# Casting the second piece of w_in on GpSimd and VectorE, half each, instead of on GpSimd alone

## The chip, the cores and the metric

One core of a Trainium2 chip. The time is device microseconds (us) of one execution. The profile is one execution taken by the hardware profiler; its span (first to last instruction) is some 1.8 us shorter than the time. A run that is over 1.5% above the fastest of its kernel would count as slow.

## The reference

Linear attention (softmax of q over the head dimension, softmax of k over the sequence), then a feed-forward pair with exact GELU. All inputs are float32.

```python
kv = np.einsum('bhsd,bhse->bhde', k_s, v)                 # q, k, v: (8, 8, 576, 64)
attn = np.einsum('bhsd,bhde->bhse', q_s, kv)
x = attn.transpose(0, 2, 1, 3).reshape(4608, 512)
h = x @ w_in                                               # w_in: (512, 2048)
out = (0.5 * h * (1 + erf(h / sqrt(2)))) @ w_out           # w_out: (2048, 512)
```

## The kernel before

In this kernel TensorE multiplies w_in in bf16, so w_in must be cast. It arrives in five pieces of columns (256, 256, 512, 512, 512), each staged in float32 as 128 partitions x 4 blocks of 128 rows (in this kernel also called head pairs, since x comes out of the attention by head pairs). GpSimd casts the first piece block by block and the second in two halves of two blocks; VectorE casts the rest, one block per instruction.

```python
    wi_cols = [256, 256, 512, 512, 512]

    def cast_wi(i, w, eng):
        n = wi_cols[i]
        r = n // 128
        o = wi_bf[:, :, wi_off[i]:wi_off[i] + n].rearrange("p d (c m) -> p d c m", c=r)
        w = w[:, :, 0:n].rearrange("p d (m c) -> p d c m", c=r)
        if eng == "p":
            for h in range(2):
                nc.gpsimd.tensor_copy(out=o[:, 2 * h:2 * h + 2], in_=w[:, 2 * h:2 * h + 2])   # L428
        else:
            for c in range(NDM):
                nc.vector.tensor_copy(out=o[:, c], in_=w[:, c])                                # L431
    ...
    for dm in range(NDM):
        cast_wi_dm(0, wi[0], dm, nc.gpsimd)          # L439, four casts of 128x256
    ...                                              # x of the first batch, its evacuation to xT
    cast_wi(1, wi[1], "p")
    ...
    h_phase(0, {0: [lambda: cast_wi(2, wi[2], "v")], ...}, groups={0: 2, 4: 4, 8: 4}, ...)
```

`h_phase` computes tiles of 128 columns of h. Tiles 0 and 1 (first piece) are interleaved, eight matmuls. Tiles 2 and 3 (second piece) follow one by one, four matmuls each, one per block. Tiles 4 to 7 read the third piece. All matmuls with w_in are at L327, those with w_out at L355.

The softmax here doesn't subtract the row's maximum and nothing guards it: scores larger than these inputs give would overflow.

Of the kernel before, what the change touches and what calls it, by code (L numbers as in the profile page):

```python
# [16 lines left out]
def kernel(  # L17
# [16 lines left out]
    nc = tc.nc  # L34
# [43 lines left out]
    def table(func):  # L78
        nc.scalar.activation(out=scr[:, 1:2], in_=scr[:, 0:1], func=func)  # L79
# [225 lines left out]
    def x_all(b):  # L305

        for hp in range(HP):
            pool, tag = (psum_h, "h") if hp < 3 else (psum_a, "a")
            x_tile(b, hp, pool, tag)
        x_mm(b, 0)  # L310
        x_mm(b, 1)
        for hp, eng in ((0, "s"), (2, "v"), (1, "s"), (3, "v")):
            x_evac(b, hp, eng)

    def x_evac(b, hp, eng="v"):
        ps = st[b][f"x{hp}"]
        if eng == "v":
            nc.vector.tensor_copy(out=st[b]["xT"][:, hp, :], in_=ps)  # L318
        else:
            nc.scalar.copy(out=st[b]["xT"][:, hp, :], in_=ps)  # L320
# [88 lines left out]
    def load_wi(i):  # L409

        w = wst.tile([128, NDM, 512], FP32, tag="w")
        n = wi_cols[i]
        src = moe_w_in[:, wi_off[i]:wi_off[i] + n].rearrange("(c p) f -> p c f", p=128)
        d = NDM // wi_parts[i]
        for c in range(0, NDM, d):
            nc.sync.dma_start(out=w[:, c:c + d, 0:n], in_=src[:, c:c + d])
        return w
# [3 lines left out]
    def cast_wi(i, w, eng):  # L421
        n = wi_cols[i]
        r = n // 128
        o = wi_bf[:, :, wi_off[i]:wi_off[i] + n].rearrange("p d (c m) -> p d c m", c=r)
        w = w[:, :, 0:n].rearrange("p d (m c) -> p d c m", c=r)
        if eng == "p":
            for h in range(2):
                nc.gpsimd.tensor_copy(out=o[:, 2 * h:2 * h + 2], in_=w[:, 2 * h:2 * h + 2])  # L428
        else:
            for c in range(NDM):  # L430
                nc.vector.tensor_copy(out=o[:, c], in_=w[:, c])  # L431
# [53 lines left out]
    wi = [load_wi(i) for i in range(5)]  # L485
# [43 lines left out]
    x_mm(0, 1)  # L529
    x_evac(0, 2, "s")  # L530
    x_evac(0, 3)
    cast_wi(1, wi[1], "p")
    table(AF.Gelu)

    def ybank():
# [4 lines left out]
    def a2bank(i):  # L540
# [3 lines left out]

    h_phase(0, {
        0: [lambda: cast_wi(2, wi[2], "v")],
        2: [lambda: cast_wi(3, wi[3], "v")],
        6: [lambda: cast_wi(4, wi[4], "v")],
        9: [lambda: cast_wo(0, wo[0])],
# [91 lines left out]
    for c in range(2, B + 1):  # L641
# [19 lines left out]
        if c < B:  # L661
            w = [lambda c=c: x_all(c + 1)]
# [34 lines left out]
```

## Time and profile before

| | before |
|---|---|
| time, first 3 runs | 279.69 us median, 279.55 to 280.07 |
| profiled execution | 279.73 us, span 277.9 us |
| TensorE busy | 271.6 us, 98% of the span |
| GpSimd's two casts of the second piece | 0.64 and 1.05 us |
| TensorE's gap before tile 2's third matmul | 0.435 us, of which 0.216 is the usual spacing |

How to read it: in the groups and the timeline a row is start, length, engine, line, operation, tiles, shapes and count; a bracket at the end gives idle time of the engine and what ended it. PE is TensorE's matmuls, PEld its weight loads, DVE is VectorE, POOL is GpSimd. L431 is line 431 of that run's kernel, so an edit moves the numbers a little: the casts of the third piece are L431 before and L432 in the changed kernel. The chain of waits follows the last instruction back through what released each step; only time on this chain can be won.

### The profile page before, as it was taken

How to read it: one execution, taken by the hardware profiler on the slowest of the kernel's cores; microseconds unless marked ns; L12 is line 12 of the kernel's file. 1: busy time of each engine (PE TensorE's matmuls, PEld its weight loads, DVE VectorE, ACT ScalarE, POOL GpSimd, SP SyncE). 2: the span in 40 equal slices, each digit the busy share in tenths (PEclk: the TensorE clock that was granted, in tenths of full speed). 3: DMA queues.
4: the chain of work that ended last, by engine and by line, in shares of the span. 5: the costliest groups of instructions: out<-in, count | busy, mean ns of one | idle time of the engine just before them, and what ended most of it. 6: DMA issues, size and time to landing. Idle time of an engine off the chain costs nothing.

```text
span 277.9 us, 4563 instructions
## 1 busy us (share of the span) xinstructions
PE 271.6 (98%) x1918; PEld 126.1 (45%) x1918; DVE 100.6 (36%) x153; ACT 157.9 (57%) x246; POOL 33.4 (12%) x27
## 2 busy tenths in 40 slices
PE   7799999999999999999999999999999999999995
PEld 3444454444444444444444444444444444444443
DVE  2876574319743540093008400651015200130012
ACT  4867675789377816791569246943683363136400
POOL 1530041002020220014000500050005000000000
PEclk9999999999999999999999999999999999999999
DMA  7999999963992148712981199117502500220033
GB/s 249 396 400 429 398 400 407 398 251 100 297 341 60 68 107 255 294 38 87 247 346 41 43 234 389 46 49 189 115 0 75 151 2 0 75 78 0 0 78 77
DMA packets 44981, 50.10 MB, mean 180 GB/s; under 512 B 20385, under 2 KB 29857, under 8 KB 44705
## 3 DMA queue, kind: packets, MB, share of 16 engines
q1 hardware_dynamic: 44560, 49.39, 53.2%
q10 hardware_dynamic: 400, 0.43, 0.6%
q8 instruction: 15, 0.25, 0.4%
q14 instruction: 6, 0.04, 0.1%
HBM read 36.70 MB, written 9.44 MB: 166 GB/s over the span
## 4 chain that ended last, share of the span: by engine, by line
PE 93%; DMA 4%; POOL 1%; ACTq 0%; SPq 0%; issue 0%; DVE 0%
PE ps L355 44%; PE ps L327 43%; DMA w<-in_moe_w_in_dram 2%; DMA touch<-in_moe_w_in_dram 2%; PE kv L199 2%; PE ps L294 1%; PE ps L380 1%; PE pair L327 1%; POOL wi_bf L428 1%; POOL wi_bf L439 1%; PE ps L299 0%; PE tp L255 0%; ACTq L482 0%; PE ps L255 0%; ACTq L101 0%; SPq L103 0%
## 5 line engine op out<-in xcount | busy, mean ns | idle before, releaser
L327 PE MATMUL ps<-xT,wi_bf 128*128 128x512 bf16 x568 | 125.1, 379 | 0.1
L355 PE MATMUL ps<-wo_bf,g 128*128 128x512 bf16 x560 | 124.2, 379 | 0.0
L333 ACT ACTIVATE g<-ps 128x512 bf16<-128x512 f32 x142 | 83.6, 598 | 67.0 <-PE ps L327 66.9
L327 PEld LDWEIGHTS <-wi_bf 128*128 128x128 bf16 x576 | 56.1, 98 | 68.2 <-POOL wi_bf L428 0.5
L355 PEld LDWEIGHTS <-g 128*128 128x128 bf16 x560 | 53.9, 98 | 64.3 <-issue 0.4
L363 DVE COPY y_sb<-ps 128x512 f32<-128x512 f32 x33 | 22.6, 686 | 81.0 <-PE ps L355 80.6
L238 POOL TENSOR_TENSOR e<-e,recq 128x2048 bf16<-128x2048 bf16 (+1 forms) x9 | 25.7, 2856 | 175.3 <-DVE recq L237 147.2
L162 DVE CAST v_aug<-f 128x576 bf16<-128x576 f32 x24 | 16.4, 745 | 48.8 <-DMA f<-in_v_dram 48.8
L236 DVE TENSOR_REDUCE qsum<-e 128x16 f32<-128x1024 bf16 (+1 forms) x13 | 21.1, 1620 | 13.9 <-ACT e L145 13.9
L320 ACT CAST xT<-ps 128x512 bf16<-128x512 f32 x18 | 9.9, 588 | 28.1 <-PE ps L294 18.1
L145 ACT ACTIVATE e<-f 128x512 bf16<-128x512 f32 (+1 forms) x42 | 20.5, 556 | 3.2 <-DMA f<-in_q_dram 3.0
L150 ACT ACTIVATE ek<-f 128x2304 bf16<-128x2304 f32 (+1 forms) x10 | 17.2, 1728 | 0.6 <-DMA f<-in_k_dram 0.6
L318 DVE CAST xT<-ps 128x512 bf16<-128x512 f32 x17 | 11.0, 685 | 17.0 <-PE ps L294 14.1
L79 ACT ACT_TABLE_LOAD x9 | 11.5, 1283 | 2.8 <-issue 2.6
L472 PE MATMUL ps<-zeros 128*128 128x512 f32 x14 | 8.6, 779 | 1.4 <-DVE zeros L497 1.4
L145 ACT ACT_TABLE_LOAD x7 | 9.0, 1283 | 0.1
L431 DVE CAST wi_bf<-w 128x512 bf16<-128x512 f32 x12 | 7.4, 648 | 2.2 <-DMA w<-in_moe_w_in_dram 2.0
L199 PEld LDWEIGHTS <-ek 64*64 64x64 bf16 x576 | 6.4, 105 | 2.7 <-issue 0.6
L199 PE MATMUL kv<-v_aug,ek 64*64 64x65 bf16 x576 | 6.8, 193 | 0.5 <-POOL v_aug L162 0.5
L238 DVE TENSOR_TENSOR e<-e,recq 128x1024 bf16<-128x1024 bf16 x4 | 6.3, 1565 | 0.1
L472 PEld LDWEIGHTS ps<-zeros 128*128 128x128 f32 x14 | 3.5, 258 | 5.7 <-issue 4.3
L294 PE MATMUL ps<-qT,kvc 64*64 64x512 bf16 x62 | 5.4, 389 | 0.4 <-DVE kvc L218 0.4
(37 smaller groups left out, 49.9 us busy)
## 6 DMA issues: line engine op xcount, KB each, us to landing
out_dram<-y_sb SPq DMA_DIRECT2D x32, 256.0 KB, 2.4
f<-in_k_dram SPq DMA_DIRECT2D x6, 1152.0 KB, 10.2
f<-in_v_dram SPq DMA_DIRECT2D x6, 1152.0 KB, 11.8
f<-in_q_dram SPq DMA_DIRECT2D x6, 1024.0 KB, 7.2
w<-in_moe_w_in_dram SPq DMA_DIRECT2D x6, 512.0 KB, 8.6
f<-in_v_dram SPq DMA_DIRECT2D x8, 288.0 KB, 6.6
f<-in_q_dram SPq DMA_DIRECT2D x4, 512.0 KB, 8.8
w<-in_moe_w_out_dram SPq DMA_DIRECT2D x2, 1024.0 KB, 11.6
```

The costliest lines, as they stand in the source:

```text
L79: nc.scalar.activation(out=scr[:, 1:2], in_=scr[:, 0:1], func=func)
L145: nc.scalar.activation(out=dst[:, i], in_=src[:, u], func=AF.Exp)
L150: nc.scalar.activation(out=ek[b % 2][:, i:i + n], in_=st[b]["kf"][:, i:i + n].rearrange("p x (n d) -> p x n d", n=NS), func=AF.Exp,)
L162: eng.tensor_copy(out=o, in_=i)
L199: nc.tensor.matmul(st[b]["kv"][hp][c, 0:D + 1], ek[b % 2][pr, hp, n, :], v_aug[b % 2][pr, hp, n, 0:D + 1], start=(n == 0), stop=(n == NS - 1),
L236: nc.vector.reduce_sum(out=qsum, in_=eq[:, :, hs, :], axis=AX.X)
L238: eng.tensor_tensor(out=eq[:, :, hs, :], in0=eq[:, :, hs, :], in1=recq.unsqueeze(3).to_broadcast([128, J, w, D]), op=ALU.mult,)
L327: nc.tensor.matmul(ps, wi_bf[:, dm, t * 128:(t + 1) * 128], st[c]["xT"][:, dm, :], start=(dm == 0), stop=(dm == NDM - 1),)
L333: nc.scalar.activation(out=st[c]["g"][:, t, :], in_=ps, func=AF.Gelu)
L355: nc.tensor.matmul(ps, st[c]["g"][:, t, j * 128:(j + 1) * 128], wo_bf[:, t, :], start=(t == 0), stop=(t == NDF - 1),)
L363: nc.vector.tensor_copy(out=y_sb, in_=ps)
L472: nc.tensor.matmul(ps, z[:, 0:128], z, start=True, stop=True)
```

## The change

The intent is to have the second piece ready sooner: two engines cast it side by side, and VectorE does its half before it turns to the third piece.

```diff
-        if eng == "p":
-            for h in range(2):
-                nc.gpsimd.tensor_copy(out=o[:, 2 * h:2 * h + 2], in_=w[:, 2 * h:2 * h + 2])
+        if eng == "pv":
+
+            nc.gpsimd.tensor_copy(out=o[:, 0:2], in_=w[:, 0:2])
+            nc.vector.tensor_copy(out=o[:, 2:4], in_=w[:, 2:4])
...
-    cast_wi(1, wi[1], "p")
+    cast_wi(1, wi[1], "pv")
```

## The prediction

> **What bounds the kernel now.** I read the page first: which engine is busy, what the chain of waits holds.
>
> ```profile
> span 277.9 us, 4563 instructions
> PE 271.6 (98%) x1918; PEld 126.1 (45%) x1918; DVE 100.6 (36%) x153; ACT 157.9 (57%) x246; POOL 33.4 (12%) x27
> ...
> PE 93%; DMA 4%; POOL 1%; ACTq 0%; SPq 0%; issue 0%; DVE 0%
> PE ps L355 44%; PE ps L327 43%; DMA w<-in_moe_w_in_dram 2%; DMA touch<-in_moe_w_in_dram 2%; PE kv L199 2%; PE ps L294 1%; PE ps L380 1%; PE pair L327 1%; POOL wi_bf L428 1%; POOL wi_bf L439 1%; PE ps L299 0%; PE tp L255 0%; ACTq L482 0%; PE ps L255 0%; ACTq L101 0%; SPq L103 0%
> ```
>
> TensorE (PE) is busy 98% of the span and is 93% of the chain. Vector, Scalar and GpSimd engines have room. The only compute on the chain that is not TensorE's is GpSimd's: the casts of w_in at L439 and L428, 1% each. L428 is the line that the change touches. So next the chain of waits in order of time, between 10 and 30 us (start, length, what):
>
> ```profile
> 13.27 0.05 issue
> 13.32 1.48 POOL wi_bf L439 x4
> 14.80 1.59 POOL wi_bf L428 x2
> 16.40 0.05 issue
> 16.45 5.35 PE ps L327 x24
> ```
>
> GpSimd casts the first piece of w_in in four instructions, then the second in two, and when the last of these ends TensorE goes on. From 16.45 us to the end the chain names TensorE alone (in its part after 46 us no other engine has over 0.1%, until the last copy). Hence what is won at 16.45 us is won at the end, as long as no other wait takes the place; what is won elsewhere is worth nothing. But the chain's 1.59 us for L428 is not what can be won: TensorE worked most of that time. How long it stood still, the timeline says, read in short windows so that rows are not merged:
>
> ```profile
> 16.01 0.38 PE L327 MATMUL ps<-xT,wi_bf 128*128 128x512 bf16 x1
> ...
> 16.44 0.55 PEld L327 LDWEIGHTS <-wi_bf 128*128 128x128 bf16 x4 [0.55 <-POOL wi_bf L428]
> ...
> 16.45 0.39 PE L327 MATMUL ps<-xT,wi_bf 128*128 128x512 bf16 x1
> ```
>
> Undisturbed, these matmuls start 0.216 us apart (ten starts from 14.06 to 16.01 give 1.95 / 9; 48 in the 10.36 us of the chain after 28.27 give the same). The one after 16.01 should have started at 16.226 and started at 16.445. **The stall is 0.22 us.** The 0.55 us before the weight load is mostly the usual idle time of a loader that is one matmul ahead. Which matmul is it? Tiles 0 and 1 are run interleaved, eight matmuls; then tile 2, one head pair after another. The stalled one is tile 2's third: head pair 2, the first to read the second half of the second piece. Last, the casts around it:
>
> ```profile
> 14.20 0.69 DVE L318 CAST xT<-ps 128x512 bf16<-128x512 f32 x1
> ...
> 14.75 0.64 POOL L428 CAST wi_bf<-w 128x512 bf16<-128x512 f32 x1
> ...
> 15.25 0.62 DVE L431 CAST wi_bf<-w 128x512 bf16<-128x512 f32 x1 [0.36 <-DMA w<-in_moe_w_in_dram]
> ...
> 15.34 1.05 POOL L428 CAST wi_bf<-w 128x512 bf16<-128x512 f32 x1
> ...
> 15.89 0.97 DVE L431 CAST wi_bf<-w 128x512 bf16<-128x512 f32 x1
> ```
>
> VectorE finishes its last evacuation of xT at 14.89 and waits until 15.25 for the third piece. GpSimd's second cast takes 1.05 us where its first took 0.64, and VectorE's next takes 0.97 where the median of the 12 is 0.62.
>
> **What the Trainium skill says.** (1) "SBUF — State Buffer", section "Who interferes with whom": VectorE in a two-port mode and GpSimd hold a shared port pair as an exclusive lock for the whole instruction; who issues first has it, the other blocks fully. "Copy" and "cast" are listed as able to enter such a mode. The trace agrees: the second GpSimd cast overlaps a VectorE cast that began 0.09 us before it and ends 0.40 us later than its sibling would; the VectorE cast after it is longer by 0.35 us. (2) "VectorE: DVE Perf Modes", "Mode 2×_2P — use both read ports for one tensor": source and destination in SBUF, and an outermost dimension that is even. The new half has two head pairs outermost, so I take it for a two-port cast too. (3) "Perfetto Trace Analysis", "GPSIMD Engine Instruction": a GpSimd span is unreliable, and the spacing of starts is better. Starts here are 0.59 us apart, so 0.64 is not far off, and TensorE's release 0.05 us after the recorded end of 16.39 backs that end.
>
> **The change part by part.** The order of instructions on each engine, compared: GpSimd has one L428 cast instead of two; VectorE has one more cast of 128x512, between the xT evacuation and the 12 casts of L431; the others are unchanged, except that tile 2's third weight load now waits for VectorE. No bytes, transfers or matmuls change.
>
> Removed: GpSimd's second cast, 1.05 us, of which about 0.40 us is waiting. Its first stays where it was, 14.75 to 15.39, so tile 2's first two matmuls, from 15.79 on, have their weights in time.
>
> Added: one VectorE cast. The second piece landed at 14.62 by the record of its transfer, so the cast can start when VectorE is free, about 14.91. Alone it takes 0.62 us, to 15.53. But GpSimd has had the ports since 14.75, so I expect it to be held, as the VectorE cast at 15.89 was: that one ended 0.47 us after GpSimd's end (16.86 less 16.39). The same after 15.39 gives 15.86; with 0.05 us for the semaphore, 15.91. The matmul is due at 16.226, and in the trace before it started with its weight load (16.44 and 16.45), so I count a stall only from there. The whole stall goes, with 0.3 us to spare; with 0.1 if the load has to keep its usual lead of one matmul, at 16.01.
>
> Moved: the casts of the third piece. The first starts near 15.88 instead of 15.25, but no GpSimd cast is left to collide with: three casts of 0.62 us end near 17.75, where they ended at 17.40. The fourth waits for its data (landed 18.50) in both kernels. TensorE reads the first in tile 4, which it reaches after six more matmuls: 16.226 + 6 x 0.216 = 17.52, one us after it is ready (16.50). The second is ready at 17.12 and wanted at 18.38, the third at 17.75 and wanted at 19.25. All are hidden.
>
> Transfers: the staging buffer of the second piece comes free earlier, but the transfer that reuses it is issued at 16.64, right after another one landed at 16.58, not after the cast at 16.39. I expect it to stay there. The next, at 19.17, follows the third piece's fourth cast, which doesn't move.
>
> Then the waits further on, where a TensorE that is 0.22 us early might meet something that didn't move. Fourth piece: ready 20.23 for 20.98. Last piece: ready 24.49 for about 25.1. First cast of w_out: ready 27.19 for 28.05. Transposes of the second batch: VectorE's normalisation ends 38.02, TensorE comes at 38.41. Its v: GpSimd's last cast ends 42.84, TensorE comes at 43.19. The smallest margin is some 0.35 us, above the 0.22 us that is taken from it. So nothing should absorb the gain.
>
> Sum: 279.69 - 0.22 + 0 = **279.47 us**, 0.08% less.
>
> **Rivals.**
> A. VectorE's half ends late: the port pair changes hands more slowly, or its 64-column pattern is slower than L431's. If it ended at 16.30 instead of 15.86, TensorE would go on at 16.35 instead of 16.45, and the gain would be 0.1: 279.6. For it: both overlapping casts in this trace came out long. Against: their added 0.35 to 0.40 us is in my sum already.
> B. VectorE gets the ports first, or both get half speed. If VectorE holds them from 14.91 to 15.53, GpSimd's half ends 0.52 us later (as at 16.39, after 15.87), at 16.05; with the semaphore 16.10, and tile 2's first matmul, due at 15.79, stalls by 0.31. The 0.22 is saved and 0.31 lost: 279.8. For it: only 0.16 us separates the two starts, and GpSimd's depends on a transfer landing at 13.27. Against: GpSimd starts first in this trace.
> C. The gain is made and lost again at a wait tied to transfers, which are saturated until 55 us: 279.69. For it: many transfers land just ahead of use between 30 and 45 us. Against: the margins above.
> D. The extra VectorE work delays the third piece's casts until VectorE bounds the stretch. It would need over 1 us of delay, and the sum shows 0.35; nothing in the profile speaks for it.
>
> **Range and chances.** I give the main line 0.7 (279.47), A 0.12, B 0.06 and C 0.12. The weighted mean is 0.7 x 279.47 + 0.12 x 279.6 + 0.06 x 279.8 + 0.12 x 279.69 = 279.54; I say 279.5, between it and the main line. Three runs of the kernel before spread over 0.52 us, more than twice the effect, so the range is set by that spread: 279.1 to 279.9. Two per cent is 5.6 us, and the whole of the touched stretch, from the first cast to the resumed matmul, is 3.1 us; so faster by 2% is shut out, and slower by 2% would need a failure that no rival contains. Chances: 0.01, 0.98, 0.01.
>
> **What would show it.** Right: the matmuls of tile 2 run 0.216 us apart with no gap near 16.2; the page's chain has no L428 entry; the VectorE cast of L429 starts near 14.9 and ends at 15.8 to 15.9, longer than 0.62 us, while GpSimd's L428 cast keeps its 0.64; the L431 casts after it take 0.62 each; TensorE's chain from there on is unbroken and the span is 277.7. Wrong: a weight load that waits for L429 or for GpSimd at 15.6; L428 over 0.9 us long; a new gap between 17 and 45 us; or a span at 277.9 although the gap at 16.2 is gone, in which case the first displaced wait after it is the one to look for.

(The weighted mean in it should read 279.53; the slip of 0.01 changes nothing.)

## The result

| | before | changed |
|---|---|---|
| median of 6 runs | 279.59 us (279.49 to 280.07) | 279.54 us (279.43 to 279.83) |
| ratio of the means | | 0.9997, 95% interval 0.9984 to 1.001 |
| profiled span | 277.9 us | 277.7 us |
| first matmul with w_in to first with w_out | 14.054 us | 13.824 us |
| from there to the last matmul | 246.203 us | 246.207 us |

A ratio is the mean time of one kernel's fast runs over the mean of the other's fast runs of the same rounds, so it is not quite the ratio of the medians. Every interval below is a 95% interval of such a ratio.

The last two rows are differences of start times of single matmuls in the two traces. I use them below because they leave out the front of the kernel: over all 14 profiles TensorE's first matmul with w_in came anywhere between 14.02 and 14.27 us.

From the page of the changed kernel, the busy times and the chain of waits:

```profile
PE 269.6 (97%) x1890; PEld 126.3 (45%) x1918; DVE 100.7 (36%) x154; ACT 157.8 (57%) x246; POOL 32.4 (12%) x26
...
PE 93%; DMA 4%; issue 1%; POOL 0%; DVE 0%; SPq 0%
PE ps L327 44%; PE ps L355 43%; DMA f<-in_v_dram 2%; PE kv L199 2%; PE ps L294 2%; DMA f<-in_q_dram 1%; PE ps L380 1%; PE pair L327 1%; POOL v_aug L162 0%; PE ps L299 0%; PE tp L255 0%; PE ps L255 0%; SPq L103 0%; DVE kvc L218 0%; DVE y_sb L385 0%
```

The casts of w_in have left the chain. PE counts 1890 matmuls instead of 1918 only because 28 records are missing from this trace; the stretch after the first matmul with w_out is equal to 0.004 us. The 1% of "issue" goes with those missing records: the chain in order of time (start, length, what) has a piece of 0.05 us where one is missing, as at 14.92 (the pieces before 13.75 stand between a release and the next start, as at 13.27 before):

```profile
11.20 0.05 issue
11.25 0.66 POOL v_aug L162
11.91 0.05 issue
11.96 0.68 POOL v_aug L162
12.64 0.04 issue
12.68 0.50 PE kv L199 x34
...
13.75 0.41 PE ps L294 x4
14.16 0.75 PE ps L327 x3
14.92 0.05 issue
14.97 6.64 PE ps L327 x30
```

Before, this chain came in from the transfer of w_in through six GpSimd casts and handed over to TensorE at 16.45. Now it comes in through the attention of the first batch (the casts of v, the kv product, x) and is TensorE's from 13.75 on. The timeline of VectorE, GpSimd and the weight loads in that stretch:

```profile
14.74 0.63 POOL L428 CAST wi_bf<-w 128x512 bf16<-128x512 f32 x1
...
14.85 0.81 DVE L429 CAST wi_bf<-w 128x512 bf16<-128x512 f32 x1
15.58 0.61 DVE L432 CAST wi_bf<-w 128x512 bf16<-128x512 f32 x1
...
14.09 2.92 PEld L327 LDWEIGHTS <-wi_bf 128*128 128x128 bf16 x15 [0.23 <-POOL wi_bf L440]
```

VectorE's half (L429) ends at 15.66, well ahead of the matmul at 16.26 that reads it. The row of weight loads, which broke off before at 15.89 and went on at 16.44, now runs through.

So the profile gained 0.23 us where it was predicted, and carried it to the end. But the medians differ by 0.05 us. That is what the experiments were for.

### The profile page after: what moved, and what is told of

Read it like the earlier page. It is cut to its first block, busy times and chain, and to the rows that moved or that the text cites. A ratio compares the mean times of both kernels' runs of the same rounds, so it can differ in the third digit from the quotient of the medians.

```text
span 277.7 us, 4535 instructions
## 1 busy us (share of the span) xinstructions
PE 269.6 (97%) x1890; PEld 126.3 (45%) x1918; DVE 100.7 (36%) x154; ACT 157.8 (57%) x246; POOL 32.4 (12%) x26
## 4 chain that ended last, share of the span: by engine, by line
PE 93%; DMA 4%; issue 1%; POOL 0%; DVE 0%; SPq 0%
PE ps L327 44%; PE ps L355 43%; DMA f<-in_v_dram 2%; PE kv L199 2%; PE ps L294 2%; DMA f<-in_q_dram 1%; PE ps L380 1%; PE pair L327 1%; POOL v_aug L162 0%; PE ps L299 0%; PE tp L255 0%; PE ps L255 0%; SPq L103 0%; DVE kvc L218 0%; DVE y_sb L385 0%
## 5 line engine op out<-in xcount | busy, mean ns | idle before, releaser
L355 PE MATMUL ps<-wo_bf,g 128*128 128x512 bf16 x543 | 122.1, 379 | 1.6 <-issue 1.1
```

Source lines behind the costliest of these rows:

```text
L355: nc.tensor.matmul(ps, st[c]["g"][:, t, j * 128:(j + 1) * 128], wo_bf[:, t, :], start=(t == 0), stop=(t == NDF - 1),)
```

## The experiments

The three sessions ran on three chips, and the kernel before was timed in each, so each run is compared with its own session.

### Session 1: is the gain real, does a stall here reach the end, and what do the shared ports cost?

**a1_changed_again** is the changed kernel, unedited.

> The changed kernel itself, timed again in more rounds. Theory (the 0.22 us stall of TensorE before tile 2's third matmul is gone and nothing takes its place): 0.15 to 0.25 us less than the kernel before in the mean, ratio about 0.9993, and in the profile no gap near 16.2 us. Rival (the gain of the profile is chance, or is absorbed in most executions): ratio 0.9998 to 1.0002.

Measured: 279.57 us median of 5 (mean 279.588) against 279.58 (mean 279.667 of 9), ratio 0.9998, interval 0.9985 to 1.001. The profile has no gap, and 13.810 us between the two marks. So the profile answers to the theory, and the ratio to the rival. Something in the size was wrong.

**a2_before_two_more** puts two more GpSimd casts between the two halves (the loop over the halves is written out):

```diff
+            nc.gpsimd.tensor_copy(out=o[:, 0:2], in_=w[:, 0:2])
+            for _ in range(2):
+                nc.gpsimd.tensor_copy(out=spare, in_=zeros32)
+            nc.gpsimd.tensor_copy(out=o[:, 2:4], in_=w[:, 2:4])
```

> The kernel before, with two more GpSimd casts of 128x512 (of a constant tile, to a spare one) between its two casts of the second piece, so that the second half comes later. Theory (a stall at this place goes to the end in full): GpSimd's second half ends 1.2 to 1.7 us later than 16.39, the gap before tile 2's third matmul grows from 0.22 to 1.4 to 1.9, and the time grows by the same amount within 0.2 us, to 280.8 to 281.4. Rival (transfers and later waits absorb what changes here): the gap grows alike, but the time by less than half of it, under 280.4.

Measured: 281.13 us median of 4 (mean 281.085), 1.42 us over the mean of before; ratio 1.0051, interval 1.0038 to 1.0065. GpSimd's second half, started at 16.59, ended at 17.60, and the weight load waited for it:

```profile
16.59 1.02 POOL L431 CAST wi_bf<-w 128x512 bf16<-128x512 f32 x1
...
17.65 0.33 PEld L328 LDWEIGHTS <-wi_bf 128*128 128x128 bf16 x3 [1.77 <-POOL wi_bf L431]
```

The gap before the matmul is 1.654 us, so the stall is 1.654 - 0.216 = 1.44 us, and the mean time grew by 1.42. A stall here goes to the end in full; the rival, that later waits absorb it, falls. It also gives a first hint: 1.42 is the whole stall, not the stall less the 0.22 us that before should have had.

**a3_changed_two_more** puts the same two casts behind GpSimd's one cast in the changed kernel.

> The changed kernel, with the same two GpSimd casts behind its one cast of the second piece. Theory (after the change nothing that TensorE wants hangs on GpSimd behind the first half): the time of the changed kernel within 0.15 us, though VectorE's casts beside the two become longer. Rival (the shared ports make VectorE's half too late): a gap of 0.2 us or more before tile 2's third matmul and 279.75 or more.

Measured: mean 279.566, median 279.66 of 5; 13.824 us between the marks and no gap, although VectorE's next casts took 0.72 and 1.00 us beside GpSimd's. As the theory has it: GpSimd's later work no longer matters, and a 1.4 us disturbance that the kernel before passed on in full is ignored.

**a4_all_vector** gives VectorE both halves:

```diff
-            nc.gpsimd.tensor_copy(out=o[:, 0:2], in_=w[:, 0:2])
+            nc.vector.tensor_copy(out=o[:, 0:2], in_=w[:, 0:2])
```

> The whole second piece cast by VectorE, one half after the other; GpSimd has none of it. Theory (GpSimd's running cast is what lengthens VectorE's half from 0.62 to 0.81 us): both VectorE casts take 0.62 within 0.03, the second ends near 16.0, still ahead of its matmul at 16.23, and the time is that of the changed kernel within 0.15 us. Rival (the 0.81 belongs to the cast's own pattern): the L429 casts take 0.8 each, the second ends near 16.3 to 16.5, a gap of 0.1 to 0.3 us is back, and the time is that of the kernel before.

Measured: mean 279.604, median 279.65 of 5; no gap, 13.810 us. The timeline of VectorE:

```profile
14.71 0.42 DVE L428 CAST wi_bf<-w 128x512 bf16<-128x512 f32 x1
...
15.04 0.42 DVE L429 CAST wi_bf<-w 128x512 bf16<-128x512 f32 x1
...
15.38 0.62 DVE L432 CAST wi_bf<-w 128x512 bf16<-128x512 f32 x1
```

The rival falls: without GpSimd beside it the half is short, not 0.8 us. But it takes 0.42 us, not the 0.62 that I had taken from the L431 row. Beside GpSimd's cast it was 0.81, so the ports cost it 0.39 us. The one engine alone needs 0.75 us from its first start to its last end (14.71 to 15.46); the two together need 0.92 (14.74 to 15.66).

### Session 2: how large is the stall of the kernel before, and does the place on VectorE matter?

**d1, d2, d3_before_again**: the kernel before, unedited, profiled three more times.

> The kernel before, unchanged, profiled once more. Open after the first runs: the profile of before shows a stall of 0.22 us, yet the timed gain is about 0.05. Theory V (the stall varies between executions): with P the start of GpSimd's first cast of the first piece and H the start of TensorE's first matmul with w_in, the second half is ready near P + 3.12 and wanted at H + 2.17, so the stall is P - H + 0.95, or none where that is negative. In the profile of before P is 13.32 and H 14.06; in the profiles of the five other executions so far the sum would give 0.17, 0, 0, 0 and 0. So a new profile of before shows 0 to 0.1 more often than 0.22. Rival S (the stall is there in every execution and something else eats the gain): a gap of 0.2 to 0.25 us before tile 2's third matmul here too, whatever P - H is.

> As the run before this one: a second new profile of the kernel before. Theory V: the stall follows P - H + 0.95 within 0.05 us, where GpSimd's second cast is again the longer of the two; shorter where that cast gets the ports before VectorE does. Rival S: 0.2 to 0.25 us.

> A third new profile of the kernel before. Theory V: as for the two before it, and the execution with the larger P - H has the larger stall. Rival S: 0.2 to 0.25 us in all three.

Measured between the marks: 13.825 us (d1), 13.810 (d2) and 14.031 (d3), against 14.054 in the first profile of before. So d1 and d2 have no stall at all, and d3 has 0.427 - 0.216 = 0.21 us. Rival S falls. Theory V is right that the stall varies, but its formula failed: for d1, with P 13.28 and H 14.02, it gives 0.21, and there is none. (The expectation of d2 had allowed for that: less where GpSimd's second cast gets the ports before VectorE does.) What tells the four apart is in the timelines, first d3, then d1:

```profile
15.31 0.65 DVE L431 CAST wi_bf<-w 128x512 bf16<-128x512 f32 x1 [0.36 <-DMA w<-in_moe_w_in_dram]
...
15.41 1.05 POOL L428 CAST wi_bf<-w 128x512 bf16<-128x512 f32 x1
...
16.52 0.33 PEld L327 LDWEIGHTS <-wi_bf 128*128 128x128 bf16 x3 [0.54 <-POOL wi_bf L428]
```

```profile
15.29 0.66 POOL L428 CAST wi_bf<-w 128x512 bf16<-128x512 f32 x1
...
15.52 0.92 DVE L431 CAST wi_bf<-w 128x512 bf16<-128x512 f32 x1 [0.66 <-DMA w<-in_moe_w_in_dram]
```

In d3 VectorE's first cast of the third piece begins before GpSimd's second cast, and GpSimd's takes 1.05 us. In d1 the third piece landed 0.2 us later, GpSimd began first, and its cast took 0.66; VectorE's was the long one, and nobody waits for that. This made a new theory, O: the stall is lost at the shared ports, and who starts first decides.

**b2_behind_third**: VectorE casts its half after the first cast of the third piece.

```diff
             nc.gpsimd.tensor_copy(out=o[:, 0:2], in_=w[:, 0:2])
+            cast_wi(2, wi[2], "v", range(0, 1))
             nc.vector.tensor_copy(out=o[:, 2:4], in_=w[:, 2:4])
...
-        0: [lambda: cast_wi(2, wi[2], "v")],
+        0: [lambda: cast_wi(2, wi[2], "v", range(1, 4))],
```

> The changed kernel, but VectorE casts its half of the second piece behind the first cast of the third piece instead of ahead of it. Theory (the place ahead of the third piece is what brings the half in time): that first cast waits for its data near 15.25 and ends near 15.9, the half ends at 16.3 to 16.5, and the gap before tile 2's third matmul is 0.1 to 0.25 us; time 0.1 to 0.25 above the changed kernel's. Rival (only taking the half off GpSimd matters, its place on VectorE doesn't): no gap, and the changed kernel's time.

Measured: 279.72 us median of 5 (279.51 to 279.97), mean 279.758 against 279.590 for before, ratio 1.0009, interval 0.9995 to 1.0022. The profiled execution was the fastest of the five (279.51); there the half ended at 16.19 and the gap was 0.239 us, a stall of 0.02. The stall is smaller than expected since the half takes 0.42 and not 0.62 us. The mean leans to the theory, but the slower executions weren't profiled and the interval holds 1, so this one is inconclusive.

### Session 3: the order at the ports, and what bounds the start now

**e1_before_vector_waits**: GpSimd keeps both halves, and VectorE cannot start the third piece before GpSimd is done.

```diff
             for h in range(2):
                 nc.gpsimd.tensor_copy(out=o[:, 2 * h:2 * h + 2], in_=w[:, 2 * h:2 * h + 2])
+            nc.vector.tensor_copy(out=spare[:, 0:1], in_=wi_bf[:, 3, 256:257])
```

> The kernel before, GpSimd still casting both halves, but VectorE's casts of the third piece wait for GpSimd's second half (one tiny VectorE copy reads one column of it first). Theory O (the stall of the kernel before is the order at the shared ports: where VectorE's cast of the third piece starts before GpSimd's second cast, that one takes 1.05 us instead of 0.65): GpSimd's second cast takes 0.65 us within 0.03, ends 0.3 us or more before its matmul is to start or near it, no gap over 0.05 us before tile 2's third matmul, and the stretch from TensorE's first matmul with w_in to its first with w_out is 13.81 to 13.84 us as in the changed kernel. Rival W (GpSimd's amount of work is the cause, the order isn't): a gap of 0.15 us or more stays. Time: that of the changed kernel within 0.15 us.

Measured: GpSimd's second cast took 0.646 us, no gap, 13.810 us between the marks. The length is what theory O says. The missing gap does not test rival W (GpSimd has too much to do): the cast began at 15.13, and its matmul was due at 16.43, so even 1.05 us would have ended in time. What speaks against W is d1, as the table below shows. The time was 279.70 us median (mean 279.658), within the 0.15 us of a5 below (279.562) but no better than before (279.661). In its profile TensorE's first matmul with w_in came at 14.27, the latest of all; whether the edit does that or chance is open.

**e2_before_gpsimd_late**: a small cast between the halves was to make GpSimd lose the race always (the loop is written out here too).

```diff
             nc.gpsimd.tensor_copy(out=o[:, 0:2], in_=w[:, 0:2])
+            nc.gpsimd.tensor_copy(out=spare[:, 0:128], in_=zeros32[:, 0:128])
             nc.gpsimd.tensor_copy(out=o[:, 2:4], in_=w[:, 2:4])
```

> The opposite: the kernel before with one small GpSimd cast (128x128 of a constant tile) between its two halves, so that VectorE's first cast of the third piece has always begun when GpSimd's second half begins. Theory O: GpSimd's second cast takes 0.95 to 1.1 us in the profile and ends at 16.5 to 16.8, the gap is 0.3 to 0.6 us more than the spacing of 0.216, and the time is 0.25 to 0.55 us above the kernel before. Rival W: the cast takes 0.65 and the gap and time grow only by the small cast's 0.2 to 0.25 us or less.

The expectation missed: in the profiled execution GpSimd won the race, by 11 ns (15.300 against 15.311), because it had begun on the first piece at 13.04 instead of 13.32.

```profile
15.30 0.63 POOL L430 CAST wi_bf<-w 128x512 bf16<-128x512 f32 x1
...
15.31 1.11 DVE L433 CAST wi_bf<-w 128x512 bf16<-128x512 f32 x1 [0.45 <-DMA w<-in_moe_w_in_dram]
```

It is the sharpest evidence for theory O all the same: with a lead of 11 ns GpSimd's cast kept its 0.63 us and VectorE's took 1.11. There was no gap. The five timed runs (279.55 to 280.03, mean 279.742, ratio 1.0003) show no clear difference, so the forecast of 0.25 to 0.55 us more, for a race that GpSimd always loses, stays untested.

**c1_last_v_split**: in the changed kernel the cast that its chain hangs on is split over two engines.

```diff
-    cast_v(0, 3, nc.gpsimd)
+    o = v_aug[0][:, 3, :, 0:D]
+    i = st[0]["vf"][:, 3, :].rearrange("p (n d) -> p n d", n=NS)
+    nc.gpsimd.tensor_copy(out=o[:, 0:5], in_=i[:, 0:5])
+    nc.vector.tensor_copy(out=o[:, 5:9], in_=i[:, 5:9])
```

> The changed kernel, with the cast that its chain now hangs on shortened: the last piece of the first batch's v is cast in two parts, 5 of 9 blocks by GpSimd and 4 by VectorE. Theory (after the change TensorE's start with w_in is set by the landing of that piece at 11.9 us and the 0.67 us cast behind it, and from there everything is TensorE): the first matmul with w_in starts 0.1 to 0.2 us earlier relative to that landing (2.19 us after it now), the time falls by as much against the changed kernel beside it. Rival (the two parts block each other at the shared ports, or VectorE's norms come late by as much): no change within 0.1 us.

Measured: mean 279.568 against 279.562 for the changed kernel beside it: nothing gained, so the theory missed. The part of GpSimd's took 0.46 us and ended at 12.15, but the first matmul with w_in came at 14.20, which is 2.56 us after the landing instead of less than 2.19. The chain there shows another limit, the first piece of w_in:

```profile
13.05 1.13 POOL wi_bf L440 x3
14.18 0.03 issue
14.20 7.50 PE ps L327 x34
```

**a5_changed_third**: the changed kernel once more, on this chip.

> The changed kernel once more, to have it on the same chip and in the same rounds as the other three. Theory: no gap before tile 2's third matmul, 13.81 to 13.84 us from the first matmul with w_in to the first with w_out, and a mean 0.05 to 0.15 us below the kernel before, since the kernel before has its stall of about 0.22 us in some executions only (in two of the four profiled ones). Rival: a gap here as well.

Measured: no gap, 13.823 us; mean 279.562 (279.57 median of 5) against 279.661 (279.64 of 9), 0.10 us less; ratio 0.9996, interval 0.9982 to 1.001. As the theory has it, with the caution that the interval holds 1.

## Why the prediction was right or wrong

The time (279.54 for 279.5), the range and the verdict were right. That alone tells little: the outcomes that the prediction gives to its main line and to the rivals A, B and C (279.47 to 279.8) all lie within its range of 279.1 to 279.9. The steps:

**The stall of 0.22 us.** Right for the trace it was read from, and wrong as a property of the kernel. This is the term of the sum that was mis-sized: "279.69 - 0.22". Start times, lengths and stalls in microseconds, from the traces in which GpSimd casts both halves and VectorE's third-piece cast follows freely:

| execution | GpSimd's second cast | VectorE's first of the third piece | first | stall |
|---|---|---|---|---|
| before | 15.343, 1.046 | 15.254, 0.620 | VectorE by 0.089 | 0.22 |
| d3 | 15.415, 1.053 | 15.312, 0.645 | VectorE by 0.103 | 0.21 |
| e2 | 15.300, 0.634 | 15.311, 1.109 | GpSimd by 0.011 | 0 |
| d2 | 15.055, 0.643 | 15.212, 0.962 | GpSimd by 0.157 | 0 |
| d1 | 15.288, 0.660 | 15.517, 0.918 | GpSimd by 0.229 | 0 |

Who comes second takes 0.3 to 0.5 us longer. GpSimd's start hangs on the landing of the first piece, VectorE's on that of the third, and their order changes from one execution to the next. a2, left out of the table since its extra casts come in between, agrees: GpSimd's second half began 0.49 us after a cast of VectorE's and took 1.02 us.

The order alone does not make the stall; GpSimd's lead over TensorE counts too. Had the second cast taken 1.05 us in the last three rows (its start, plus 1.05, plus 0.05 for the release, against the time at which the matmul was due: 16.33, 16.19 and 16.19), the stall would have been 0.07 us in e2, none in d2 and 0.20 in d1. So d1 is the execution that shows the order at work: P - H is -0.74 there, -0.73 in before and -0.77 in d3, GpSimd's work is the same, and only the order differs.

I had read the 0.40 us of waiting inside GpSimd's 1.05 correctly, and didn't ask whether it is always there. With the stall in two of the four profiles of before, an estimate of the mean gain is 0.22 x 2/4 = 0.11 us. The means of the three sessions with the changed kernel differ by 0.09 (279.657 and 279.563 from the six runs each of the result), 0.08 and 0.10. They agree with the estimate, but each interval holds 1, and four profiles are few: that the change saves 0.1 us on average is likely and not shown. (All 24 runs of before against all 16 of the changed kernel, resampled within their sessions after the fact, give 0.09 us, 95% interval 0.02 to 0.17: an estimate that leans the same way.) What is shown is that the stall doesn't occur in the three profiles of the changed kernel.

**The base.** 279.69 was the median of three runs; of six it is 279.59. The base was 0.1 too high and the gain 0.1 too large, so the sum came out close partly by luck.

**VectorE's half.** Predicted from about 14.91 to 15.86; measured 14.85 to 15.66. The mechanism, being held by GpSimd's cast, was right (0.42 alone, 0.74 to 0.81 beside it). In the three profiles of the changed kernel, and in a3 and c1, it ended 0.28 to 0.29 us after GpSimd's cast, however early it had begun. The size was off: I took 0.62 us alone, and 0.47 after GpSimd's end, from L431's casts. The same number of elements in another pattern took 0.42 (a4).

**Rival A and rival B.** A was too pessimistic; the half had 0.6 us to spare. B (VectorE first at the ports) did not come up in any of the changed kernel's profiles: GpSimd led by 0.11 to 0.19 us each time.

**The third piece's casts.** Right: 0.61 us each and hidden. One part was wrong: the fourth block landed at 17.26 instead of 18.50, and the transfer of w_out behind it was issued at 17.93 instead of 19.17. That changed no wait on TensorE. In a1 the fourth cast started at 18.68 and in a5 at 17.34, and in e1, where GpSimd casts both halves, at 17.48, so it varies within and across the two programs.

**Transfers.** Right: the transfer that reuses the second piece's buffer was issued at 16.68, after another landing at 16.61, as before.

**Rival C, a later wait that eats the gain.** Not in the profiled pair (246.203 and 246.207 us after the first matmul with w_out). But the smallest margin that I listed, 0.35 us for the second batch's v, isn't safe: in d1 that v was cast by 43.17 instead of 42.83, TensorE's kv products took 0.66 us instead of 0.51, and the same stretch took 246.416 us. In a3 it took 246.322; in the other 12 profiles 246.20 to 246.21. So such waits exist in some executions of both programs; d1 had no stall at w_in and lost 0.21 us there.

## What to carry to other kernels

A gap read from one trace is a sample: before a gain is booked, ask which two arrivals decide the gap, and profile the unchanged kernel a few more times. Where GpSimd and VectorE both cast in SBUF, the order of two starts can be worth more than the split of the work: here one VectorE working alone needed 0.75 us for both halves, and the two engines side by side 0.92 to 0.94. And measure a short stretch between two marks in the trace where the whole time is too noisy: it resolved 0.02 us here, while the medians could not resolve 0.1.

## What the Trainium skill lacked or had wrong

- "SBUF — State Buffer", "Who interferes with whom": the exclusive lock and "whoever issues first" are borne out, by the recorded starts and in one case down to a lead of 11 ns. A blocked VectorE cast ended a nearly constant time after GpSimd's, 0.28 to 0.29 us at L429 and 0.46 to 0.49 at the third piece's casts, as a full block would have it. The section gives no times for two casts: in these runs the second comer took 0.40 us longer on GpSimd (1.05 for 0.65) and 0.30 to 0.49 longer on VectorE (0.92 to 1.11 for 0.62).
- The same section says that a VectorE instruction with at most one SBUF input outside the two-port modes does not contend with GpSimd. The L431 casts start 0.53 us apart for 512 elements per partition, which at the 0.96 GHz of "VectorE: DVE Perf Modes", "Specifications", is an estimate of one element per cycle, half of what the next point's mode gives; and they do contend. Whether they are two-port casts that run at half pace, or the rule has a gap, no run here tells.
- "VectorE: DVE Perf Modes", "Mode 2×_2P — use both read ports for one tensor": the page gives two results per cycle, and the conditions listed hold for both patterns of 512 elements, but the one that reads every second element took 0.42 us (starts 0.33 apart) and the one that reads every fourth 0.62 (0.53 apart). Those conditions do not tell the two apart. That the source's step is the reason is my reading of the difference; it was not tested by itself.
- No page says how much the order at the ports varies between executions of one program: VectorE came first by 0.10 us at most and GpSimd by up to 0.23 in five profiles.
